# A fused attention and gated feed-forward kernel: first tile's first layer by halves of the contraction, tiny matmuls on zeros, four transpositions moved

## The chip, the core and the metric

The kernel runs on one core of a Trainium2 chip. The metric is the device time of one execution in microseconds (us). A core has TensorE (PE in the profile; PEld is its loading of weights), VectorE (DVE), ScalarE (ACT), GpSimd (POOL) and SyncE (SP), each with a queue of its own that it works through in order; they wait for one another by semaphores. Transfers are issued by GpSimd and SyncE here.

## What is computed

```python
scores = scale * np.matmul(q, k.transpose(0, 1, 3, 2))      # 8 batches, 8 heads, 576 rows, 64 columns
mask = (rel >= 0) & (rel < 64)                               # a causal window of 64
attn = softmax of scores under the mask
x = np.matmul(attn, v), heads side by side: 4608 x 512
gate = np.maximum(x @ w_gate, 0.0)                           # 512 x 1536
val = x @ w_val
return (gate * val @ w_out).astype(np.float32)               # 1536 x 512
```

## The kernel before, in words

The attention works on units of 192 rows; two units make a tile of the feed-forward part (384 rows for tiles 0 to 3, 512 for later ones). For a unit, TensorE makes scores in banks of PSUM (`u_st`, L265), ScalarE their exponentials (`u_exp`, L299), VectorE multiplies them by the mask (`u_mask`, L306; units 0 and 1 have a bias in the bank instead, `bias_mm`, L232), TensorE multiplies by v (`u_pv`, L336), VectorE divides (`u_recip`, L350, `u_norm`, L357) and transposes into the tile `xt` (`u_turn`, L379). In unit 1 ScalarE divides the second half of the heads (L369). `xt` has four slices of 128 along the contraction; heads 0 to 3 give slices 0 and 1, heads 4 to 7 slices 2 and 3.

The first layer of tiles 0 and 1 is `hidden` (L557). It goes over the 12 blocks of 128 columns of the two weights `wg` and `wv`: four matmuls (one for each slice, L589) fill a block's columns of a bank. ScalarE makes the relu of a `wg` bank (L572) and VectorE multiplies it by the `wv` bank (`gate`, L575). The banks of `hidden` are numbers 0 to 3 in turn (`one_bank`), and a bank is written again only when its relu or gate has read it. Tile 0 runs blocks 0 to 3 for its two units apart (192 columns, two blocks to a bank), then blocks 4 to 11 for both (384 columns, one block to a bank). Later tiles use another scheme (`fast_hidden`, L634), which multiplies fewer matrices.

Weights come in three parts of four blocks, each as two transfers issued by GpSimd (`w_load`, L159): slices 0 and 1, then slices 2 and 3. Ahead of some of them in GpSimd's queue stand copies that spread v over partitions (`v_spread`, L215).

The order of issue is written out by hand. `Weaver` holds a heap of actions with due times and a clock; each block of matmuls adds its estimated time (4 x (columns + 7) / 2400 us), and `W.advance` issues what has become due. `w_done` says when a part of the weights is taken to have landed: 15.2, 17.7, 20.3, 22.8, 27.0 and 29.6. The scores of unit 2 are due at 23.2, its exponentials at 24.0 and 0.4 apart, its masks at 24.45 and 0.4 apart, its values at 27.4; a relu or gate falls due when its bank's last matmul has been issued. The second batch's k and q are transposed by four instructions of VectorE (`qk_trans`, L199), due at 31.6 and 1.4 apart. The clock only fixes the order in each queue; when an instruction runs, semaphores and landings decide.

Before the first layer TensorE has matmuls on zeros (`keep_hot`, L229, and `heat`, L226): they add nothing to a result. The zeros are made by VectorE (L1088).

Of the kernel before, what the change touches and what calls it, by code (L numbers as in the profile page):

```python
# [47 lines left out]
def kernel(  # L48
# [10 lines left out]
    nc = tc.nc  # L59
# [4 lines left out]
    U = 192  # L64
    UB = S // U
    NU = B * UB
    NC = DM // 128
    NF = DF // 128
    G = 4
    scale = 1.0 / float(D) ** 0.5  # L70
    TT = 2 * U
# [55 lines left out]
    def band_bias():  # L127

        nc.vector.tensor_scalar(bias, mask, 30000.0, -30000.0, MUL, mybir.AluOpType.add)
        return 0.0  # L130
# [10 lines left out]
    W = Weaver()  # L141
    units = {}
# [3 lines left out]
    def xt_tile(t):  # L146
        if t not in xts:
            xts[t] = x_sb.tile([128, NC, WT], FP16, name="xt")
        return xts[t]


    w_done = {}

    def w_load(wt, src, f0, f1, landed):

        if wt is not wo:
            ns = slice(128 * f0, 128 * f1)
            for a in range(2):
                nc.gpsimd.dma_start(wt[:, 2 * a:2 * a + 2, ns], src.rearrange("(a p e) n -> a p e n", a=2, e=2)[a, :, :, ns])  # L159
        if wt is wo:  # L160
            nc.gpsimd.dma_start(wo[:, f0:f1], src.rearrange("(c p) n -> p c n", p=128)[:, f0:f1])
        w_done.update(((wt.name, f), landed) for f in range(f0, f1))

    def w_need(wt, f):
        while (wt.name, f) not in w_done:
            W.pop()
        W.advance(w_done[wt.name, f])

# [17 lines left out]
    def first_round(name, copies):  # L188
        n = S // 32 * D // len(copies)
        to = nat[0, name, 0] = nats[:, 2 * "kq".index(name)]  # L190
        for i, copy in enumerate(copies):
            copy(to[:, n * i:n * i + n], nat["32", name][:, n * i:n * i + n])

    def qk_trans(b, name, hh, j0=0, j1=S // 32):

        src = nat[b, name, hh].bitcast(FP32).rearrange("p (j e) -> p j e", e=32)
        dst = qTs[b % 2][:, hh] if name == "q" else kTs[b % 2][:, hh, 64:64 + S]
        dst = dst.bitcast(FP32).rearrange("p c o -> p (c o)")
        nc.vector.transpose(dst.rearrange("p (i j) -> p j i", i=32)[:, j0:j1], src[:, j0:j1])  # L199
# [23 lines left out]
    def heat(n, to, start=True):  # L223

        for _ in range(n):
            nc.tensor.matmul(to, zero[:, 0:128], zero[:, 0:to.shape[1]], start=start, stop=start, skip_group_check=not start)  # L226

    def keep_hot(to):
        nc.tensor.matmul(to, zero32[:, 0:128], zero32[:, 0:to.shape[1]], start=False, stop=False, skip_group_check=True)  # L229
# [6 lines left out]
    def one_bank():  # L236
        taken["one"] += 1
        to = singles[(taken["one"] - 1) % 4]
        while id(to) in unread:
            W.pop()  # L240
        return to
# [34 lines left out]
    def u_bias(u):  # L276

        st_tiles(u)
        for c in range(G):
            bias_mm(units[u]["st"][c])  # L280
        units[u]["biased"] = True
# [125 lines left out]
    def part_written(banks):  # L407
        written.update((id(to), 0) for to in banks)
# [145 lines left out]
        while normed[0] < n:  # L554
            W.pop()

    def hidden(t, spans, f0=0, f1=NF, each=1):  # L557

        if t not in gs:
            gs[t] = g_sb_p.tile([128, NF, WT], FP16, name="g_sb"), {}  # L560
        g_sb, done = gs[t]
        xt = xt_tile(t)
        n = spans[0][1] - spans[0][0]

        w = 512 // n
        each = max(each, w)

        def part(tile):
            return tile[:, 0:w * n].rearrange("p (w n) -> p w n", w=w)

        def relu(r_sb, h1):
            nc.scalar.activation(part(r_sb), part(h1), ACT.Relu)  # L572

        def gate(f, c0, r_sb, h2):
            nc.vector.tensor_tensor(g_sb[:, f:f + w, c0:c0 + n], part(r_sb), part(h2), MUL)  # L575
            done.update(dict.fromkeys(range(f, f + w), c0 + n))

        for fb in range(f0, f1, each):
            r2s = [f_sb.tile([128, 2, WT], FP32, name="pr", bufs=4) for _ in range(2)]
            r_sbs = {}  # L580
            for i, wt in enumerate((wg, wv)):
                for c0, f in ((c0, f) for c0, _ in spans for f in range(fb, fb + each, w)):
                    h = one_bank()
                    part_written([h])
                    for b in range(w):
                        W.advance(W.clock)
                        w_need(wt, f + b)
                        for c in range(NC):
                            nc.tensor.matmul(h[:, b * n:b * n + n], wt[:, c, (f + b) * 128:(f + b) * 128 + 128],  # L589
                                             xt[:, c, c0:c0 + n], start=(c == 0), stop=(c == NC - 1))  # L590
                        W.clock += 4 * (n + 7) / 2400.0
                    if i == 0:
                        r_sb = r_sbs[c0, f] = r2s[len(r_sbs) // 2][:, len(r_sbs) % 2]
                        W.at(W.clock, lambda r_sb=r_sb, h=h: relu(r_sb, h))
                    else:
                        W.at(W.clock, lambda f=f, c0=c0, r_sb=r_sbs[c0, f], h=h: gate(f, c0, r_sb, h))

    def fast_hidden(t, seven=None):

# [418 lines left out]
    def out_mm(t, op, sub, f):  # L1018
        g_sb, done = gs[t]
        while done.get(f, 0) < sub * 128 + 128:  # L1020
            W.pop()
        w_need(wo, f)
        nc.tensor.matmul(op, g_sb[:, f, bass.ds(sub * 128, 128)], wo[:, f],  # L1023
                         start=(f == 0), stop=(f == NF - 1))
        W.clock += 519 / 2400.0
# [48 lines left out]
    with tc.manual_schedule():  # L1074
# [14 lines left out]
        zero = zero32.bitcast(FP16)  # L1089
        st_tiles(0)  # L1090
        bands()
        v_load(0, ((1, 0, 128), (3, 0, 64)))
        v_load(1, ((3, 64, 128), (5, 0, 128)))
        w_load(*G3[0], 15.2)
        w_load(*V3[0], 17.7)
        k_zeros()
        band_bias()

        first_round("k", (dve, act))
        u_bias(0)  # L1100
        u_bias(1)
# [22 lines left out]
        for hh in range(2):  # L1124
            u_pv(1, (hh,), True)
        heat(1, units[1]["st"][3])
        for hh in range(2):
            u_recip(1, (hh,))
        u_norm_act(1, 1)
        u_norm(1, 0)  # L1130
        for hh in range(2):
            u_turn(1, (hh,))
        w_load(*G3[1], 20.3)
        w_load(*V3[1], 22.8)
        v_load(2)
# [13 lines left out]
        for u in (4, 5):  # L1149
            v_load(u)  # L1150
        for i, (name, hh) in enumerate((n, hh) for n in "kq" for hh in range(2)):
            W.at(31.6 + 1.4 * i, lambda name=name, hh=hh: qk_trans(1, name, hh))
        for hh, T in enumerate((36.6, 38.8)):
            W.at(T, lambda hh=hh: u_st(3, (hh,)))
            for i in range(G):
# [93 lines left out]
                pass  # L1249

        W.advance(15.3)
        hidden(0, ((0, U), (U, TT)), 0, 4, 4)
        hidden(0, ((0, TT),), 4, NF, 4)
        hidden(1, ((0, U),), each=4)
        output(0, (0, 1), (0, 8, NF))
        ready(1)
# [78 lines left out]
```

## Time and profile before

| | us |
|---|---|
| median of 3 runs | 302.06 (301.67 to 302.10) |
| the profiled execution | 302.04 |
| its span, first to last instruction | 300.3 |
| TensorE busy | 289.6 (96%) |
| VectorE busy | 251.7 (84%) |
| ScalarE busy | 196.0 (65%) |
| GpSimd busy | 201.7 (67%) |

A line of the timeline has the start and the length in us, the engine, the line of the kernel, the operation, what it writes and reads, the shape and the count of instructions merged; a bracket holds the engine's idle time before it and what ended that. The granted clock of TensorE is 1.0 throughout. In the window from 32 to 42 us TensorE is busy without a gap, and VectorE for 1.97 to 2.00 of every 2 us.

### The profile page before, as it was taken

To read this page: it belongs to the slowest core of one execution; us is meant where nothing else is said; L and a number is where in the kernel's file an instruction comes from. 1 tells how busy PE (TensorE), PEld (TensorE's weight loads), DVE (VectorE), ACT (ScalarE), POOL (GpSimd) and SP (SyncE) were. 2 spreads that over 40 slices of the span, in tenths; PEclk is the share of its full clock that TensorE was granted. 3 is DMA by queue.
4 is the path that set the end of the run, shared out by engine and by line. 5 is a ranking of instruction groups with operands and counts; after the bars stand their busy time and mean duration, and the time that the engine had idled before them with its cause. 6 is when DMAs were issued, how large, how long until landed. Compare 5 with 4: busy or idle time off the path is not lost.

```text
span 300.3 us, 11073 instructions
## 1 busy us (share of the span) xinstructions
PE 289.6 (96%) x4643; PEld 239.4 (80%) x4643; DVE 251.7 (84%) x517; ACT 196.0 (65%) x408; POOL 201.7 (67%) x241
## 2 busy tenths in 40 slices
PE   4899999999999999999999999999999999999994
PEld 2475877748957975888888888888888888888894
DVE  5947895997995999789999899989858985896584
ACT  3545336258848848885798579857985698538850
POOL 8767689868957893985957595759375617441750
PEclk9999999999999999999999999999999999999999
DMA  7999999979919636911399239922911210031013
GB/s 216 183 196 194 194 197 179 160 131 241 80 40 181 164 70 149 146 42 38 61 219 120 60 53 219 126 57 53 173 37 35 74 41 0 3 103 41 0 38 105
DMA packets 59506, 33.20 MB, mean 111 GB/s; under 512 B 39552, under 2 KB 53824, under 8 KB 59456
## 3 DMA queue, kind: packets, MB, share of 16 engines
q0 software_dynamic: 46688, 18.29, 52.3%
q1 hardware_dynamic: 12192, 13.75, 15.1%
q8 instruction: 36, 0.59, 0.8%
q10 hardware_dynamic: 576, 0.46, 0.5%
q14 instruction: 14, 0.11, 0.1%
HBM read 37.75 MB, written 9.44 MB: 157 GB/s over the span
## 4 chain that ended last, share of the span: by engine, by line
PE 87%; DMA 5%; POOL 4%; DVE 2%; issue 1%; DVEq 0%; POOLq 0%
PE bank L634 46%; PE bank L847 17%; PE bank L589 7%; PE bank L767 5%; PE bank L1023 5%; PE bank L265 3%; DMA wg<-in_moe_w_gate_dram 3%; PE bank L465 2%; DMA v<-in_v_dram 2%; POOL v L205 1%; PE bank L336 1%; POOL wg L159 1%; DVE g_sb L659 1%; DVE g_sb L797 0%; POOL wv L159 0%
## 5 line engine op out<-in xcount | busy, mean ns | idle before, releaser
L659 POOL TENSOR_TENSOR g_sb<-pr 128x512 f16<-128x512 f32 (+1 forms) x36 | 42.7, 1193 | 43.6 <-ACT pr L676 43.6
L670 DVE TENSOR_TENSOR pr<-bank,pr 128x512 f32<-128x512 f32 (+1 forms) x96 | 58.5, 649 | 3.6 <-PE bank L634 1.9
L653 ACT COPY pr<-bank 128x512 f32<-128x512 f32 (+1 forms) x96 | 49.1, 566 | 13.7 <-PE bank L634 13.5
L659 DVE TENSOR_TENSOR g_sb<-r,bank 128x512 f16<-128x512 f32 (+1 forms) x48 | 31.3, 652 | 23.8 <-ACT r L703 22.4
L847 PEld LDWEIGHTS <-g_sb 128*128 128x128 f16 x444 | 41.8, 98 | 5.2 <-issue 0.2
L634 PE MATMUL bank<-xc,vs 128*128 128x256 f16 (+1 forms) x288 | 41.3, 266 | 0.0
L634 PE MATMUL bank<-xc,us 128*128 128x256 f16 (+1 forms) x288 | 41.3, 266 | 0.0
L634 PEld LDWEIGHTS <-vs 128*128 128x128 f16 x384 | 36.5, 98 | 3.5
L634 PEld LDWEIGHTS <-us 128*128 128x128 f16 x384 | 36.5, 98 | 3.3
L205 POOL DMA_DIRECT2D v<-in_v_dram x41 | 34.7, 866 | 2.2 <-DMA nats<-in_q_dram 1.0
L676 ACT ACTIVATE pr<-pr 128x512 f32<-128x512 f32 (+1 forms) x48 | 29.3, 610 | 9.8 <-DVE pr L670 9.8
L703 ACT ACTIVATE r<-bank 128x512 f32<-128x512 f32 (+1 forms) x48 | 27.7, 577 | 4.8 <-PE bank L634 4.0
L634 PEld LDWEIGHTS <-wg 128*128 128x128 f16 x288 | 27.4, 98 | 3.2
L634 PEld LDWEIGHTS <-wv 128*128 128x128 f16 x288 | 27.4, 98 | 2.6
L634 PE MATMUL bank<-xt,wg 128*128 128x256 f16 (+1 forms) x192 | 27.5, 266 | 0.0
L634 PE MATMUL bank<-xt,wv 128*128 128x256 f16 (+1 forms) x192 | 27.5, 266 | 0.0
L797 POOL TENSOR_TENSOR g_sb<-g_sb,xus 128x512 f16<-128x512 f16 x24 | 27.1, 1148 | 0.0
L847 PE MATMUL bank<-wo,g_sb 128*128 128x256 f16 (+1 forms) x222 | 26.6, 270 | 0.0
L430 ACT ACTIVATE pw<-bank 128x512 f16<-128x512 f32 x48 | 25.3, 605 | 1.1 <-PE bank L265 0.7
L847 PE MATMUL bank<-wts,g_sb 128*128 128x256 f16 (+1 forms) x222 | 25.4, 270 | 0.2 <-DVE xw L484 0.2
L643 ACT COPY bank<-bank 128x512 f32<-128x512 f32 (+1 forms) x48 | 24.6, 553 | 0.0
L572 ACT ACTIVATE pr<-bank 128x384 f32<-128x384 f32 x24 | 11.9, 501 | 15.5 <-PE bank L589 12.5
(107 smaller groups left out, 559.8 us busy)
## 6 DMA issues: line engine op xcount, KB each, us to landing
out_dram<-o_sb SPq DMA_DIRECT2D x30, 256.0 KB, 3.1
nats<-in_k_dram POOLq DMA_DIRECT2D x15, 288.0 KB, 6.1
nats<-in_q_dram POOLq DMA_DIRECT2D x15, 288.0 KB, 8.0
v<-in_v_dram POOLq DMA_DIRECT2D x31, 128.0 KB, 8.2
v<-v SPq DMA_DIRECT2D x27, 66.0 KB, 2.7
v<-v SPq DMA_DIRECT2D x13, 132.0 KB, 2.5
wg<-in_moe_w_gate_dram POOLq DMA_DIRECT2D x6, 256.0 KB, 6.4
wv<-in_moe_w_val_dram POOLq DMA_DIRECT2D x6, 256.0 KB, 8.1
```

The source lines that it names most:

```text
L205: nc.gpsimd.dma_start(v16s[b % 2][lo:hi, g, :, 0:64], v[b, :, 64 * g - 64 + lo:64 * g - 64 + hi].rearrange("h p d -> p h d"))
L430: nc.scalar.activation(d["p"][g].rearrange("p n c -> p (n c)"), d["st"][g], ACT.Exp, scale=scale)
L589: nc.tensor.matmul(h[:, b * n:b * n + n], wt[:, c, (f + b) * 128:(f + b) * 128 + 128], xt[:, c, c0:c0 + n], start=(c == 0), stop=(c == NC ...
L634: nc.tensor.matmul(to[:, HT * m:HT * m + HT], w[:, k, 128 * m:128 * m + 128], x[:, k], start=(first and m == 0 and k == 0), stop=(k == 1), ...
L643: nc.scalar.copy(at[j, "B", i][:, 0:TW], at[j, "A", i][:, 0:TW])
L653: nc.scalar.copy(pr[:, i], at[j, "A", i][:, 0:TW])
L659: eng.tensor_tensor(gh[:, f:f + 2, h], pair(r), pair(v), MUL)
L670: nc.vector.tensor_tensor(pr[:, i], to[:, 0:TW], pr[:, i], ADD)
L676: nc.scalar.activation(pr[:, 0], pr[:, 0], ACT.Relu)
L703: nc.scalar.activation(r, to[:, 0:TW], ACT.Relu)
L797: eng.tensor_tensor(to, x, y, op)
L847: nc.tensor.matmul(at[key][:, QN * m * whole:QN * m * whole + n1 - n0], A[:, 128 * m:128 * m + 128], B[:, c, n0:n1], start=(first and m == ...
```

## The change

The first layer of tile 0 runs by halves of the contraction. A group takes its banks together, two for `wg` in blocks 0 to 3, four otherwise; first all its blocks get slices 0 and 1, then all get slices 2 and 3. Only the first matmul of a bank starts the accumulation for the whole bank. The halves have due times of their own in `w_done`, the first 1.3 before the second. Tile 1 runs as before.

Sixteen matmuls on zeros, with 4 columns of weights and 4 columns of data, go into the first bank of blocks 8 to 11 ahead of their first matmul. Another 112 of them stand ahead of the bias turns of unit 0. The four transpositions of k and q fall due at 31.9, 32.8, 34.4 and 35.8 instead of 31.6, 33.0, 34.4 and 35.8.

```diff
-        w_done.update(((wt.name, f), landed) for f in range(f0, f1))
+        w_done.update(((wt.name, f, a), landed - 1.3 * (1 - a)) for f in range(f0, f1) for a in range(2))
...
-            nc.tensor.matmul(to, zero[:, 0:128], zero[:, 0:to.shape[1]], start=start, stop=start, skip_group_check=not start)
+            nc.tensor.matmul(to, zero[:, 0:to.shape[0]], zero[:, 0:to.shape[1]], start=start, stop=start, skip_group_check=not start)
...
-    def hidden(t, spans, f0=0, f1=NF, each=1):
+    def hidden(t, spans, f0=0, f1=NF, each=1, halves=False):
...
+                items = [[(c0, f) for f in range(fb, fb + each, w)] for c0, _ in spans]
+                if halves and i == 1:
+                    items = [sum(items, [])]
+                for group in items if halves else [[item] for items_ in items for item in items_]:
+                    hs = [one_bank() for _ in group]
+                    part_written(hs)
+                    if (fb, i, n) == (8, 0, TT):
+                        heat(16, hs[0][0:4, 0:4])
+                    for cs in ((0, 1), (2, 3)) if halves else (range(NC),):
+                        for (c0, f), h in zip(group, hs):
+                            for b in range(w):
+                                W.advance(W.clock)
+                                w_need(wt, f + b, cs[-1] // 2)
+                                for c in cs:
+                                    nc.tensor.matmul(h[:, b * n:b * n + n], wt[:, c, (f + b) * 128:(f + b) * 128 + 128],
+                                                     xt[:, c, c0:c0 + n], start=(c == 0 and not (halves and b)), stop=(c == NC - 1),
+                                                     skip_group_check=halves)
+                                W.clock += len(cs) * (n + 7) / 2400.0
...
+        heat(112, units[0]["st"][0][0:4, 0:4])
         first_round("k", (dve, act))
...
-            W.at(31.6 + 1.4 * i, lambda name=name, hh=hh: qk_trans(1, name, hh))
+            W.at((31.9, 32.8, 34.4, 35.8)[i], lambda name=name, hh=hh: qk_trans(1, name, hh))
...
-        hidden(0, ((0, U), (U, TT)), 0, 4, 4)
-        hidden(0, ((0, TT),), 4, NF, 4)
+        hidden(0, ((0, U), (U, TT)), 0, 4, 4, True)
+        hidden(0, ((0, TT),), 4, NF, 4, True)
```

More of the change, by code (lines that the diff above doesn't have):

```diff
@@ L161, in w_load, with w_need @@
             nc.gpsimd.dma_start(wo[:, f0:f1], src.rearrange("(c p) n -> p c n", p=128)[:, f0:f1])
-        w_done.update(((wt.name, f), landed) for f in range(f0, f1))
-    def w_need(wt, f):
-        while (wt.name, f) not in w_done:
+        w_done.update(((wt.name, f, a), landed - 1.3 * (1 - a)) for f in range(f0, f1) for a in range(2))
+    def w_need(wt, f, a=1):
+        while (wt.name, f, a) not in w_done:
             W.pop()
-        W.advance(w_done[wt.name, f])
+        W.advance(w_done[wt.name, f, a])
     nat = {}
@@ L581, in hidden @@
             for i, wt in enumerate((wg, wv)):
[L582 to L596, printed above, removed]
+                items = [[(c0, f) for f in range(fb, fb + each, w)] for c0, _ in spans]
@@ new lines, in hidden @@
+                if halves and i == 1:
[15 more added lines that the diff above has]
+                                W.clock += len(cs) * (n + 7) / 2400.0
+                            if cs[-1] < NC - 1:
+                                continue
+                            if i == 0:
+                                r_sb = r_sbs[c0, f] = r2s[len(r_sbs) // 2][:, len(r_sbs) % 2]
+                                W.at(W.clock, lambda r_sb=r_sb, h=h: relu(r_sb, h))
+                            else:
+                                W.at(W.clock, lambda f=f, c0=c0, r_sb=r_sbs[c0, f], h=h: gate(f, c0, r_sb, h))
```

## The prediction

> **What bounds the kernel now.** The first slice of the page shows TensorE at 96% of the span, so a change at the start counts only through the idle time of TensorE that it takes away, or adds. The list of TensorE's waits gives nearly all of it:
>
> ```profile
> PE bank L232 <- DVE bias L129: 4.4, 1, 4.4
> PE bank L589 <- DMA wg<-in_moe_w_gate_dram: 0.7, 2, 0.4
> PE bank L589 <- DVE xt L379: 0.7, 1, 0.7
> ```
>
> The timeline of TensorE says where they lie (start, length, in brackets the idle time before):
>
> ```profile
> 13.84 0.33 PE L589 MATMUL bank<-xt,wg 128*128 128x192 f16 x2
> 14.51 1.33 PE L589 MATMUL bank<-xt,wg 128*128 128x192 f16 x14 [0.35 <-DMA wg<-in_moe_w_gate_dram]
> 16.50 1.48 PE L589 MATMUL bank<-xt,wg 128*128 128x192 f16 x16 [0.66 <-DVE xt L379]
> 20.45 2.76 PE L589 MATMUL bank<-xt,wg 128*128 128x384 f16 x16
> 26.24 0.49 PE L589 MATMUL bank<-xt,wg 128*128 128x384 f16 x2
> 27.09 0.50 PE L589 MATMUL bank<-xt,wg 128*128 128x384 f16 x2 [0.36 <-DMA wg<-in_moe_w_gate_dram]
> ```
>
> The first layer idles 0.35 + 0.66 + 0.36 = 1.37 us: the most that halves can save, since from 28 us on TensorE has no idle time worth naming. Starts in the timeline are one matmul's pitch apart: 0.083 us for 192 columns (16.50 to 17.82, 16 of them), 0.163 for 384 (20.45 to 23.07), 0.49 for a unit's scores or values. What evacuates the banks lies in the timeline of VectorE and of GpSimd:
>
> ```profile
> 24.56 0.56 DVE L575 TENSOR_TENSOR g_sb<-pr,bank 128x384 f16<-128x384 f32 x1 [3.28 <-PE bank L589]
> 25.03 0.98 DVE L306 TENSOR_TENSOR p<-p,mask 128x384 f16<-128x384 f16 x1
> 26.20 0.54 DVE L575 TENSOR_TENSOR g_sb<-pr,bank 128x384 f16<-128x384 f32 x1
> 26.67 0.35 DVE L306 TENSOR_TENSOR p<-p,mask 128x384 f16<-128x384 f16 x1
> 24.76 1.04 POOL L215 COPY v<-v 64x1024 f16<-64x1024 f16 x1
> ```
>
> A mask takes 0.35; the one issued at 25.03 took 0.98 and ended at 26.01, just behind GpSimd's copy (24.76 to 25.80). At 38.41 (0.79 for 0.25) and 40.55 (0.74) it is the same, each ending 0.11 to 0.12 behind a GpSimd operation. A gate, which reads a bank, isn't held (24.56 lies inside the copy from 24.10). Today the first gate of blocks 4 to 7 stands ahead of all masks, with the due times 24.445 and 24.45.
>
> **The halves, step by step.** Start 13.84: eight matmuls on the first half take 0.66, to 14.50; the second half landed at 14.47 (landings are an issue's start and its time to landing: 8.13 + 6.3 here, 17.31 + 8.5 and 18.00 + 9.0 for the last of wg, 19.07 + 9.3 and 20.34 + 9.3 for the last of wv), so the 0.35 goes and the group ends at 15.17. What is late next is unit 1's turn: its first half ends at 15.53, and 0.12 later (as 16.38 to 16.50 now) eight matmuls run to 16.31; the second half starts at 16.50 as before, but has 8 left, not 16: 17.16 against 17.82. The 32 of wv (2.66) end at 19.82, before 20.45: **-0.65**. Relus (0.38 apart) and landings (16.43, 17.51) are in time.
>
> Now four banks end together. Gates follow each other by 0.47 (27.20: two in 1.00); a gate starts 0.275 behind its bank's last matmul. They end at 19.64, 20.11, 20.58, 21.04, TensorE wants the banks at 19.82, 20.14 and 0.33 on: with 0.1 for the handover the fourth starts at 21.14, the second half ends 0.33 + 1.30 later, at 22.77, where now it is 23.15. Of the 0.65, **0.38** is left. Scores of unit 2 to 23.25, wv of blocks 4 to 7 (landed 22.34, 23.20) to 25.86.
>
> **Where it turns.** The clock that orders the issue is arithmetic: 15.3, plus 2 x 2.653 and 2.607, is 23.213; plus 0.58 for the scores, 23.793; the first halves of wv add 1.303. So the gates of blocks 4 to 7 fall due at 25.42, 25.75, 26.07, 26.40, and the masks, due 24.45, 24.85, 25.25, 25.65, come first: VectorE's queue becomes mask, mask, mask, gate, mask, gate, gate, gate. ScalarE makes the last relu at 23.13 and the exponentials end at 24.00, 24.37, 24.74, 25.11. Mask 0 runs at 24.05, ahead of the copy whose data land at 24.04; that copy then ends at 24.90, mask 1 at 25.19, the second copy at 26.1, mask 2 at 26.4, and the first gate only at **26.88**; mask 3 27.14, the other gates 27.61, 28.08, 28.55. TensorE waits 1.1 us for bank 0, not for the weights (landed 25.78). Blocks 8 to 11 then start at 27.38, 27.71, 28.18, 28.65 (16 tiny matmuls in front), unit 2's values end at 29.46, the second half at 30.76, wv (16 x 0.163) at 33.37. Now that point is 32.57: **+0.80**.
>
> Behind it VectorE is full until 45 us (2.00 of 2.00 in nearly every window of 2 us), and the four turns of k and q (1.24 each) stand between its gates. By the new times the first stands ahead of the gate of block 11 (clock 32.153: due 31.9 before 32.153). Gates end at 33.22, 33.68, 34.15, the turn at 35.31, that gate at 35.70; TensorE wants its bank at 35.36 and gets it at 35.80: **+0.43**. Today that gate ended at 34.33, 0.25 before the bank was wanted. The later masks and the last turn can add 0 to 0.5; I take 0, since the gate of tile 1's first block moves ahead of a turn in exchange. The turns issue nothing else; what waits for them is GpSimd's next load of k into the same tile (36.60, released by a turn), with the copies behind it. Its transfer lands at 48.8 and is wanted at the next turns, due 52.0, so a us of delay is hidden there.
>
> **The 16 tiny matmuls** stand between the gates of bank 0 (26.98) and bank 1 (27.71): 0.73 less the first block's 0.33 hides 0.40, or 25 ns each. Nearest rows: 7.5 ns (48 score matmuls in 0.36, four side by side) and 83 ns (192 columns), so 0 to 0.9 more on the path; I take 0.
>
> **The 112** wait for the zeros (VectorE to 2.43) and stand ahead of the bias turns, now at 4.41. Free are 1.9 us, 17 ns each. The same two rows bound them: 0.84 to 9.3 us. I take 20 ns, the row of small ones being nearer, so 0.3 late. The bias turns run at 0.320 each, twice 0.163, and end with the two on zeros at 8.34, while the scores wait for turned q until 8.33; nothing starts sooner for a faster clock, but eight turns at 0.163 would give back 1.26, so 33 ns each stay free if the clock comes up by then. Beyond that, the wait of 1.1 for bank 0 takes up as much again: 43 ns. Value: 0. The Trainium skill, "TensorE: Matmul & The Clock Gate", section "Wait — 56ns, not 53.3ns?", states a floor of about 25 ns from start to start however small a matmul is; by it, an estimate, the 112 take 2.8 us, within what is free only if the clock rises. No run here shows such matmuls yet.
>
> **The sum.** The profiled execution is 302.04 us with a span of 300.3; the median of the runs is 302.06. 302.04 + 0.80 + 0.43 = 303.27: **303.3**.
>
> **Rivals.**
> *The masks get by.* If VectorE keeps going past the waiting second copy, mask 2 ends at 25.45 and the first gate at 25.9, but mask 3 and the next gate still stand behind that copy (27.1): wv ends at 32.86, +0.29 + 0.43, **302.75**. If nothing holds the masks, wv ends at 32.20, -0.37 + 0.43: **302.1**. For the first: at 39.12 a mask followed a mask while a copy was due; against it, the three long masks above. The Trainium skill, "SBUF — State Buffer", section "SBUF: two separate sides", says that a VectorE operation with two SBUF inputs and a GpSimd operation that reads SBUF exclude each other, the one that starts first holding the port for its whole length. By that rule the second copy, due at 24.96, goes ahead of mask 2, due behind mask 1, and the 303.3 stands.
> *The waits go and nothing takes their place: faster.* Place: the queue of VectorE at 24 to 27 us. If the gates of blocks 4 to 7 end by 26.9 (all four ahead of the masks, as the first one is today), blocks 8 to 11 run from 25.9 to 27.2, the values to 27.7, second halves to 29.0 (landed 27.05), wv (28.33, 29.60) to 31.6: -0.97, **301.1**. For it: the landings allow it, and 1.37 is there to be had. Against it: the due times. It decides by the end of the fourth gate: 0.1 + 0.33 + 0.49 + 1.30 + 2.61 = 4.83 us are left behind it, so past 27.7 nothing is saved at 32.57.
> *The 112 are slow.* From 43 ns each they delay the first scores beyond what later waits absorb; at 60 ns, 17 x 0.112 = 1.9 on top: **305.1**. Against it: the row of small matmuls.
>
> **Chances.** Forecast 0.42; masks get by, 302.75, 0.12; unhindered, 302.1, 0.20; faster, 0.18; slow 112, 0.08. A measurement here tells 0.2% (0.6 us) from no change: slower 0.42 + 0.12 + 0.08 = 0.62, same 0.20, faster 0.18. The forecast's own range is 302.8 to 304.2 (0 to 0.9 for the tiny matmuls and the small waits). To leave out no more than 2 in 10 the range reaches to the faster case: 301.0 to 304.2; outside lie the slow 112 and the best of the faster case.
>
> **What would show it.** In the profile after: no wait on a wg landing in the first layer; wv of blocks 0 to 3 ending near 19.8; three masks ahead of the gate of block 4, one of them long and ending behind the second copy; TensorE's longest wait in the first layer near 25.9, released by that gate; a wait near 35.4 released by a gate behind a turn. The prediction is wrong if that gate ends before 25.9 (then 302 or less), or if the first scores start after 8.4 by more than 1 us.

## The result, and the profile after

The changed kernel takes **303.63 us** (median of six runs, 303.34 to 303.97) against 302.06 for the kernel before (301.64 to 302.16): a ratio of 1.0057, interval 1.0044 to 1.0070. The profiled execution has a span of 301.9 us, 1.6 more than before. TensorE's waits, the list that was read first for the kernel before (engine, line, releaser: total us, how often, the longest; L596 is the line that was L589):

```profile
PE bank L226 <- DVE wts L1098: 2.5, 1, 2.5
PE bank L265 <- DVE qT L199: 0.7, 1, 0.7
PE bank L596 <- DVE g_sb L575: 0.3, 1, 0.3
PE bank L596 <- DVE xt L379: 0.3, 1, 0.3
...
PE bank L226 <- DVE g_sb L575: 0.2, 1, 0.2
```

The waits for landings of `wg` are gone, and waits for gates (`g_sb`) have come. Yet the waits of the first layer add up to less than the 1.37 us of before, so this list alone can't explain a longer time. TensorE's timeline can:

```profile
2.48 2.94 PE L226 MATMUL bank<-wts 128*4 128x4 f16 x112 [2.48 <-DVE wts L1098]
5.36 2.74 PE L232 MATMUL bank<-bias,ident 128*128 128x384 f16 x8
9.28 0.55 PE L265 MATMUL bank<-qT,kT 32*128 32x64 f16 x48
14.97 1.48 PE L596 MATMUL bank<-xt,wg 128*128 128x192 f16 x16
16.72 1.67 PE L596 MATMUL bank<-xt,wg 128*128 128x192 f16 x16 [0.27 <-DVE xt L379]
18.23 2.80 PE L596 MATMUL bank<-xt,wv 128*128 128x192 f16 x32
20.87 3.07 PE L596 MATMUL bank<-xt,wg 128*128 128x384 f16 x16
24.35 2.77 PE L596 MATMUL bank<-xt,wv 128*128 128x384 f16 x16
27.29 0.54 PE L226 MATMUL bank<-wts 128*4 128x4 f16 x16 [0.17 <-DVE g_sb L575]
...
33.77 1.48 PE L596 MATMUL bank<-xt,wg 128*128 128x192 f16 x16
36.22 0.82 PE L596 MATMUL bank<-xt,wv 128*128 128x192 f16 x8 [0.30 <-DVE g_sb L575]
```

Read it as a balance against the kernel before:
- The first scores start at 9.28 (8.38 before), the first layer at 14.97 (13.84): **+1.13**, one execution of each.
- wv of blocks 0 to 3 starts at 18.23 (17.82): the two groups ahead of it now idle 0.27, not 1.01. **-0.72**, +0.41 in all.
- wg of blocks 4 to 7 takes from 20.87 to 23.87, 3.00 instead of 2.70 (20.45 to 23.15): **+0.30**, in small pieces that no list of waits names: the handover of four banks.
- wv of blocks 4 to 7 ends at 26.96, the next matmul starts at 27.29 and the weights' ones at 27.76. From 26.96 to the end of wv of blocks 8 to 11 at 33.77 are 6.81; before, 26.24 to 32.57 were 6.33, of which 0.36 a wait for `wg`. **+0.48**.
- That makes +1.20 at 33.77. The output layer starts at 43.39 for 41.77, +1.62, and this stays: the matmuls of tile 2 begin at 70.70 for 69.08.

The queue of VectorE shows the turn:

```profile
25.05 1.73 DVE L306 TENSOR_TENSOR p<-p,mask 128x384 f16<-128x384 f16 x3 [2.95 <-ACT p L299]
26.70 0.54 DVE L575 TENSOR_TENSOR g_sb<-pr,bank 128x384 f16<-128x384 f32 x1
27.16 0.35 DVE L306 TENSOR_TENSOR p<-p,mask 128x384 f16<-128x384 f16 x1
27.43 1.47 DVE L575 TENSOR_TENSOR g_sb<-pr,bank 128x384 f16<-128x384 f32 x3
...
34.53 1.25 DVE L199 STREAM_TRANSPOSE kT<-nats 128x576 f32<-128x576 f32 x1
35.62 0.54 DVE L575 TENSOR_TENSOR g_sb<-pr,bank 128x384 f16<-128x384 f32 x1
```

Three masks stand ahead of the gate of block 4, and take 1.73 in place of 0.35 + 2 x 0.27; of these the first alone takes 1.19 (25.05 to 26.24), beside two copies of GpSimd that fill 24.32 to 26.03:

```profile
24.32 1.71 POOL L215 COPY v<-v 64x512 f16<-64x512 f16 x2 [2.93 <-DMA v<-in_v_dram]
```

### The profile page after: what moved, and what is told of

Same layout as the page of the kernel before. It is cut to its first block, busy times and chain, and to the rows that moved or that the text cites. A ratio compares the mean times of both kernels' runs of the same rounds, so it can differ in the third digit from the quotient of the medians.

```text
span 301.9 us, 11330 instructions
## 1 busy us (share of the span) xinstructions
PE 293.5 (97%) x4771; PEld 242.4 (80%) x4771; DVE 251.7 (83%) x517; ACT 195.8 (65%) x408; POOL 201.1 (67%) x241
## 4 chain that ended last, share of the span: by engine, by line
PE 90%; DVE 4%; DMA 3%; issue 1%; ACT 1%; POOL 0%; DVEq 0%; ACTq 0%; POOLq 0%
PE bank L644 45%; PE bank L857 17%; PE bank L596 9%; PE bank L777 5%; PE bank L1033 5%; PE bank L265 3%; DMA nats<-in_q_dram 3%; PE bank L465 2%; PE bank L336 2%; DVE p L306 1%; DVE g_sb L669 1%; DVE g_sb L807 0%; DVE g_sb L575 0%; DVE qT L199 0%; ACT pr L572 0%
## 5 line engine op out<-in xcount | busy, mean ns | idle before, releaser
L205 POOL DMA_DIRECT2D v<-in_v_dram x41 | 34.6, 862 | 2.9 <-DMA nats<-in_k_dram 1.4
L713 ACT ACTIVATE r<-bank 128x512 f32<-128x512 f32 (+1 forms) x48 | 27.7, 578 | 4.8 <-PE bank L644 3.9
L807 POOL TENSOR_TENSOR g_sb<-g_sb,xus 128x512 f16<-128x512 f16 x24 | 27.1, 1148 | 0.0
L572 ACT ACTIVATE pr<-bank 128x384 f32<-128x384 f32 x24 | 11.0, 497 | 15.7 <-PE bank L596 12.8
```

Source lines behind the costliest of these rows:

```text
L205: nc.gpsimd.dma_start(v16s[b % 2][lo:hi, g, :, 0:64], v[b, :, 64 * g - 64 + lo:64 * g - 64 + hi].rearrange("h p d -> p h d"))
L713: nc.scalar.activation(r, to[:, 0:TW], ACT.Relu)
L807: eng.tensor_tensor(to, x, y, op)
```

## The experiments

Each kernel was timed beside the kernel before. "First scores", "first layer" and the like are starts in TensorE's timeline of the one profiled execution. Such an execution is one sample. The kernel before, e3, e1 and e5 do the same work ahead of the first layer and agree in the first scores (8.38, 8.33, 8.40, 8.35), and yet the first layer starts at 13.84, 14.37, 14.53 and 14.71; in the last three VectorE waits longer for v to land (0.46 to 0.60, 0.27 before). So the +1.13 above is measured against the earliest of four, and a difference under 0.9 us in that start proves nothing by itself.

### What the tiny matmuls cost: e1, e2, e7, e8

e1 is the changed kernel without the 112, e2 the kernel before with the 112 alone:

```diff
-        heat(112, units[0]["st"][0][0:4, 0:4])     # e1, from the changed kernel
+        heat(112, units[0]["st"][0][0:4, 0:4])     # e2, into the kernel before
```

> The changed kernel without the 112 tiny matmuls. Theory A (VectorE's queue at 24 to 29 us sets the end of the first layer): TensorE reaches blocks 8 to 11 about 1 us sooner and waits there for the first gate, which still stands behind three masks and the GpSimd copy; the wait of 0.17 us before it grows to about 1.1, and the time falls only by what that gate comes sooner, 0.1 to 0.5 us: about 303.3 us. Theory B (the 112 delay everything): the start moves back from 14.97 to 13.84 and all of it is kept: about 302.5 us.

> The kernel before with the 112 tiny matmuls alone. They end at about 5.4 us and the first scores start near 9.2 instead of 8.38. Theory A: the later start is partly taken up by the wait for the last part of wg at 27.09, where TensorE now stands idle from 26.57; it then comes at about 27.3 with all four matmuls of the block to do, not two: 0.4 to 0.7 us, about 302.6 us. Theory B: the whole delay of 0.9 to 1.1 us stays: about 303.1 us.

Both were missed, upward. e1: **304.51** (ratio 1.0087, 1.0071 to 1.0104), 0.9 slower than with the 112. e2: **306.57** (1.0153, 1.0123 to 1.0183), so the 112 alone cost 4.5 us, nearly three times what the whole change costs. In e2's list of waits stands a releaser that the kernel before hardly has:

```profile
PE bank L336 <- issue: 0.7, 1, 0.7
PE bank L847 <- issue: 0.6, 2, 0.5
```

"issue" is time in which TensorE waits for nothing that the profile shows. It lies far from the 112; the longest stands in front of the values of a later unit (0.46 more at 205 us):

```profile
57.02 0.43 PE L336 MATMUL bank<-v,p 128*32 128x65 f16 x32 [0.74 <-issue]
```

On the page of the changed kernel a DMA queue brings instructions (packets, MB, share of the engines):

```profile
q8 instruction: 37, 0.61, 0.8%
```

In the kernel before it has 36 packets and 0.59 MB, so a packet is 16 KB. A matmul counts as two instructions on TensorE, the load of its weights and itself (4643 + 4643 on the page of before). The changed kernel has 128 pairs more, 256 instructions, and one packet more: 64 bytes each. From this came a theory: TensorE's program arrives in blocks of 256 instructions; 112 + 16 = 128 pairs are one whole block, so everything behind them keeps its place in its block, while 112 alone move each later instruction by 224, and a block's end to where TensorE has no slack. e7 and e8 test it by numbers that are otherwise alike, ahead of the bias turns in the kernel before:

```diff
+        heat(128, units[0]["st"][0][0:4, 0:4])     # e7; 16 in e8
```

> The kernel before with 128 tiny matmuls at the front instead of 112. They take 16 x 25 ns = 0.4 us more than the 112. Theory F (instructions are fetched in blocks of 16384 bytes; 128 matmuls with their weight loads are 256 instructions, a whole block, while 112 are 224 and shift every later block boundary against the work): no wait of TensorE for its own instructions, and only the later start counts: 302.6 to 303.4 us. Rival (the time of the tiny matmuls itself makes the 306.6 of the 112 alone): 306.6 us or more.

> The kernel before with 16 tiny matmuls at the front. They end at 2.9 us, before the bias turns at 4.4, so that they delay nothing. Theory F (block boundaries): 32 more instructions move every later boundary by an eighth of a block; waits of TensorE for instructions may appear, anywhere from 0 to 2 us: 302.1 to 304 us. Rival (only time at the start counts): 302.0 us.

e7: **303.10** (1.0035, 1.0023 to 1.0047), as the theory says: 16 tiny matmuls more than in e2 make it 3.5 us faster, and the list of waits has no "issue". e8: **304.17** (1.0056, 1.0035 to 1.0076), but its nine runs fall into two groups, four at 302.81 to 303.13, as in e7, and five at 304.17 to 304.93. The profiled one is the slowest: its first load of q landed at 8.97, which made the first scores 11.00, and TensorE still ran at half pace at 15.50 (two matmuls on zeros in 1.50, which take 0.91 in the kernel before at 9.16). So e8 doesn't show that 16 cost more than 128. e1 (16 alone, 32 instructions) against e3 below (none), 304.51 to 303.35, and against the changed kernel (128), 303.63, goes with the theory; its profiled execution, the slowest of five, has a wait of 1.8 us at 59 us for copies of v that came late. So a whole block is far cheaper than a part of one in e7 against e2, and the other comparisons are weaker. The "issue" waits of e2 are 1.3 of the 3.1 us by which its profiled execution (305.14) is longer than that of before (302.04).

### What the masks and the halves cost: e3, e4, e5

e3 is the halves alone: neither group of tiny matmuls, and the four turns at their old due times.

> The halves alone, without tiny matmuls and with the old due times of the four turns. Theory A: the loss is that of the halves, with the gates behind the masks: about 303.2 us, between 302.7 and 303.7. Theory B: the halves gain what the waits for weights cost, 0.4 to 1.0 us: 301.1 to 301.7 us.

e3: **303.35** (1.0038, 1.0025 to 1.0052), as expected. The halves by themselves make the kernel slower, with waits for gates as forecast. But one thing stands out. The list puts a wait of 1.2 on the turn of `xt`, and the timelines of VectorE and of TensorE say that it was no such wait:

```profile
15.48 0.58 DVE L379 STREAM_TRANSPOSE xt<-xus 128x384 f16<-128x384 f16 x1
```

```profile
17.01 1.48 PE L594 MATMUL bank<-xt,wg 128*128 128x192 f16 x16 [1.16 <-DVE xt L379]
```

The half that these matmuls read was there at 16.06; they start 0.95 later. In e5 the same turn ends at 16.41 and they start at 16.77, with the second half done only at 17.26. In the changed kernel the turn ends at 16.67 and they start at 16.72. In e1, e3 and e5 one instruction packet starts at 14.5 to 14.6 us, 2.3 to 2.4 us ahead of that start; in the changed kernel the one near by starts at 15.7.

The kernel before has the same wait. The prediction read its 0.66 at 16.50 as the wait for the second half of unit 1's turn, but the first two of these matmuls read the first half, and that was there at 15.53:

```profile
14.95 0.58 DVE L379 STREAM_TRANSPOSE xt<-xus 128x384 f16<-128x384 f16 x1
```

In e2, with the same order of matmuls, two of the 16 start with the first half (they are counted in the 18) and only 14 wait for the second:

```profile
15.29 2.07 PE L589 MATMUL bank<-xt,wg 128*128 128x192 f16 x18
17.88 1.31 PE L589 MATMUL bank<-xt,wg 128*128 128x192 f16 x14 [0.52 <-DVE xt L379]
```

The count of instructions tells what it is. Ten starts of TensorE are late without data to explain it: the three "issue" waits of e2 (57.02, 173.65, 205.05), one of 0.26 in e12 below (17.07), the first matmul of the first layer in e8 (18.25), and the first one of unit 1 in the kernel before (16.50), e1 (17.03), e3 (17.01), e5 (16.77) and e7 (18.13). Twice the number of matmuls that the trace has ahead of each is 188 or 190 more than a multiple of 256, for all ten, and an instruction packet started 2.3 to 2.6 us earlier. So these are the ends of blocks, and TensorE had run out of instructions there, though the profile itself doesn't name it; at most other ends of blocks it goes on without a pause. A whole block (e7) leaves unit 1's wait where it was.

This bears on the halves. In the kernel before, wv of blocks 0 to 3 starts 3.98 behind the first layer (17.82 less 13.84); with the halves alone in e3 3.96 (3.37 in e5); with the 112 alone in e2 3.74; with both, in the changed kernel, 3.26. The 112 ahead move the block's end from unit 1's first matmul to the first of wv (18.23), and there the packet, started 2.6 us earlier at 15.67, comes in time. So the halves win at unit 1 what was expected of them only when the block's end lies elsewhere; each of these is one execution.

e4 is the changed kernel with the masks and values of unit 2 behind the gates of blocks 4 to 7:

```diff
-        plan_exps(23.2, 2)
-        plan_values(27.4, 2)
+        plan_exps(23.2, 2, False)
+        for i in range(G):
+            W.at(26.45 + 0.05 * i, lambda i=i: u_mask(2, i))
+        plan_values(28.9, 2)
```

e5 is e3 with the same edit, the new times of the turns, and the copies of v for units 4 and 5 due at 45.5 instead of 45.6.

> The changed kernel with unit 2's four masks due at 26.45 to 26.60 and its values at 28.9, so that the four gates of blocks 4 to 7 stand ahead of the masks and the values behind the four second halves. The computation is the same. Theory A: the first gate ends near 26.8 and the others 0.47 apart without a mask between them, TensorE goes through blocks 8 to 11 without the waits, and wv of these blocks ends about 0.5 to 0.7 us sooner than 33.77: about 303.0 us, since the 112 still set its arrival at 27.0. Theory B: the order of VectorE doesn't matter, the start does: 303.6 us.

> The halves without tiny matmuls, with unit 2's masks and values behind the gates (as in the kernel with the gates first), and the copies of v for units 4 and 5 due at 45.5 instead of 45.6, so that SyncE's queue has them ahead of the first output tile, as in the kernel before. The computation is the same. Theory A (the halves lose by what is late behind them, VectorE's order first): TensorE reaches blocks 8 to 11 near 26.5 and goes through them without a wait; wv of these blocks ends near 32.4 instead of 33.8; with the wait of 0.3 to 0.5 us for the gate behind the first turn: about 302.4 us. Rival (the order of VectorE costs nothing, something else in the halves does): 303.3 us as with the halves alone.

e4: **303.81** (1.0054, 1.0041 to 1.0067); e5: **303.28** (1.0037, 1.0024 to 1.0050). In both the wait at blocks 8 to 11 is gone, but e4 is 0.18 above the changed kernel and e5 0.07 below e3, both within the spread of their runs, so both came nearer to their rivals (303.6 and 303.3). From the start of wv of blocks 4 to 7 to the end of wv of blocks 8 to 11 e4 takes 9.12 (24.85 to 33.97) where the changed kernel takes 9.42; but q landed later in the profiled execution, and its first layer started at 15.47. e5's queue of VectorE first:

```profile
26.11 1.95 DVE L575 TENSOR_TENSOR g_sb<-pr,bank 128x384 f16<-128x384 f32 x4 [4.16 <-ACT p L299]
27.98 1.16 DVE L306 TENSOR_TENSOR p<-p,mask 128x384 f16<-128x384 f16 x4
```

Four masks in 1.16, so a mask that no copy accompanies isn't long. The other traces agree. In the five kernels whose masks start more than 0.2 us before GpSimd's second copy of v ends (before, changed, e1, e3, e6), the long mask ends 0.21 behind that copy in each; in the other nine every mask takes 0.34 to 0.36. e6 and e9 below have the changed kernel's order of masks and gates, but by chance the copies end later in e6, at 26.84, and in e9 the masks start only behind them (25.78). e6 first, then e9:

```profile
24.90 2.15 DVE L306 TENSOR_TENSOR p<-p,mask 128x384 f16<-128x384 f16 x3 [2.95 <-ACT p L299]
```

```profile
26.05 1.12 DVE L306 TENSOR_TENSOR p<-p,mask 128x384 f16<-128x384 f16 x3 [2.95 <-ACT p L299]
```

Counted from the start of wv of blocks 4 to 7, the first gate is done after 3.32 in e6, 2.89 in the changed kernel and 2.39 in e9, and TensorE waits for it 0.60, 0.17 and not at all. Then e5's TensorE:

```profile
18.08 2.80 PE L594 MATMUL bank<-xt,wv 128*128 128x192 f16 x32
20.72 3.07 PE L594 MATMUL bank<-xt,wg 128*128 128x384 f16 x16
...
24.20 2.77 PE L594 MATMUL bank<-xt,wv 128*128 128x384 f16 x16
26.82 3.08 PE L594 MATMUL bank<-xt,wg 128*128 128x384 f16 x16
...
33.07 1.48 PE L594 MATMUL bank<-xt,wg 128*128 128x192 f16 x16
```

No wait is named from 18.08 to 33.07, and yet that takes 14.99, where the kernel before takes 14.75 (17.82 to 32.57) with a wait of 0.36 in it. The two groups of `wg` take 3.00 and 3.01 (20.72 to 23.72, 26.82 to 29.83) for 16 matmuls that are 2.6 long without a pause. Each follows a group of `wv` whose four banks end together; gates free them 0.47 to 0.49 apart (four in 1.95), first halves of a bank ask for them 0.33 apart. So **the halves pay 0.4 twice**, for the wait of 0.36 that they take away. That is not all that e5 loses: its output layer starts at 42.98 for 41.77, 1.21 late, of which 0.26 stand at 18.08, 0.24 come from there to 33.07, and 0.71 behind it. Of these 0.71 the gate behind the first turn makes 0.34; the rest isn't explained.

### A copy of v issued late: e6

By the new clock the output's store was issued ahead of the copies of v for units 4 and 5, and the last of these landed at 56.70 (51.17 before), 0.14 ahead of the values that read it. In e1, where it landed at 59.19, TensorE waited 1.8 us. e6 is the changed kernel with those copies first:

```diff
-            W.at(45.6, lambda u=u: v_spread(u))
+            W.at(45.5, lambda u=u: v_spread(u))
```

> The changed kernel with the copies of v for units 4 and 5 due at 45.5 instead of 45.6, which puts them ahead of the first output tile in SyncE's queue. In the changed kernel the last of them lands at 56.70 and the values want it at 56.84; with the old order it should land near 52. Theory A (that queue order only takes the reserve): 303.3 to 303.6 us, no run with a wait at 57 to 59. Rival (the order in SyncE's queue is a main part of the loss): below 303.0 us.

e6: **303.90** (1.0057, 1.0044 to 1.0070). The late copies aren't what the change costs, and the rival falls. What the changed kernel has is little reserve: 0.14 us of slack.

### The start: e9, e10, e11, e12

The 112 outlast the release of the bias turns (4.36) by 1.0 us, and the first scores are 0.90 late. If the first makes the second, zeros written earlier mend both:

```diff
+        zero32 = wts.rearrange("p a f n -> p (a f n)").bitcast(FP32)[:, 0:384]
+        nc.vector.memset(zero32, 0.0)
         for i in range(2):
             v_fixed(i, nc.vector)
-        zero32 = wts.rearrange("p a f n -> p (a f n)").bitcast(FP32)[:, 0:384]
-        nc.vector.memset(zero32, 0.0)
```

e9 is the changed kernel with this; e10 has e4's edit and e6's as well; e11 is e10 with the turns due at 32.6, 33.4, 34.6 and 35.8; e12 is e7 with the zeros early.

> The changed kernel, with the zeros written by VectorE ahead of the constant columns of v, so that the 112 tiny matmuls can begin near 1.4 us instead of 2.48 and, at 25.4 ns each, be done at about 4.3, before the bias turns are released at 4.36. Theory S (what the 112 cost in the changed kernel is the 0.95 us by which they outlast the wait for the bias): bias turns start at 4.4, first scores near 8.4 instead of 9.28, first layer near 14.0; the masks then hold the gates of blocks 4 to 7 as before, so TensorE waits some 0.7 to 1.0 us at the first of blocks 8 to 11, and the total falls only by 0.2 to 0.6, to 303.0-303.4. Rival (the loss behind the start is not made by the 112 but by later landings of k, q and instructions): first scores stay at 9.1 or later and the total stays at 303.5 or above.

> The same, with the masks and values of unit 2 issued behind the gates of blocks 4 to 7 and the copies of v for units 4 and 5 due at 45.5, ahead of the output's store. If the three terms found so far (112 too late by 0.95, the gates behind the held masks, the boundary of the instruction blocks moved away) are the whole account, the start is as in the kernel before, the halves bring their gain, nothing waits at blocks 8 to 11, wv of blocks 8 to 11 ends near 32.0 (32.57 before), and with 0.3 left for the gate behind the turn the total is 301.6 to 302.0. Rival (the start stays late for another reason): wv ends at 33 or later, total 303 or above.

> The same as the one before, with the four turns of k and q due at 32.6, 33.4, 34.6 and 35.8, so that the first stands behind the gate of block 11. If the wait of 0.3 near 35 to 36 us is that turn ahead of that gate, it goes, and the time is 0.1 to 0.3 lower. Rival: both first turns now stand ahead of the first gates of tile 1, the wait moves there, and the time is the same.

> The kernel before, with 128 tiny matmuls ahead of the bias turns and the zeros written ahead of the constant columns of v. 128 at 25.4 ns from about 1.4 last to 4.65, 0.3 past the release of the bias turns. If all that the 128 cost at the front (303.10 for 302.09 with late zeros) is their length past that release, the time is 302.2 to 302.5 and the first layer starts near 14.1. Rival (the cost comes from instruction transfers beside the first loads): first layer at 14.8 or later and 302.8 or above.

e9: **303.47** (1.0062, 1.0039 to 1.0086); e10: **303.71** (1.0059, 1.0041 to 1.0078); e11: **303.61** (1.0055, 1.0035 to 1.0075); e12: **302.57** (1.0027, 1.0009 to 1.0045). The theory fell: in e9 the first scores come after 9.1, as its rival had it, and the total lies between the two. e9's TensorE:

```profile
1.43 2.94 PE L226 MATMUL bank<-wts 128*4 128x4 f16 x112 [1.43 <-DVE wts L1096]
4.40 2.72 PE L232 MATMUL bank<-bias,ident 128*128 128x384 f16 x8
...
9.14 0.55 PE L265 MATMUL bank<-qT,kT 32*128 32x64 f16 x48 [1.37 <-DVE qT L199]
```

The bias turns start at 4.40, as before; the scores still at 9.14, after 1.37 of waiting for turned q. What makes q late is in VectorE's timeline, here for the kernel before and then for e9:

```profile
4.71 0.55 DVE L192 CAST nats<-vs 128x576 f16<-128x576 f32 x1 [0.35 <-DMA vs<-in_k_dram]
```

```profile
5.48 0.50 DVE L192 CAST nats<-vs 128x576 f16<-128x576 f32 x1 [1.13 <-DMA vs<-in_k_dram]
```

The chain from there to the turn of q (7.07 before, 7.83 in e9) is the same and begins 0.77 later, with the landing of the first k. In the changed kernel it begins 0.35 later (cast at 5.06), waits 0.24 for ScalarE's half of the cast and has a second cast of 0.78 for 0.45: 0.90 together with the handovers. So with the 112 the scores are late, but not by the length of the 112. e12 gains 0.5 on e7, with first scores at 8.98 for 9.71 and the first layer at 15.03, as the rival had it; what is left to the kernel before is 0.56, where 0.1 to 0.4 was expected and 0.7 or more by the rival, so neither theory had it whole.

Two of these profiles need a reservation. In e9 and e10 the granted clock of TensorE fell to 0.5 for 3.4 us, from 13.83 and from 11.30, and in none of the other profiles did it fall there. So the first layer of e9, at 15.96, and of e10, at 15.50, are late by this too; e11, without it, starts at 15.03.

e10 and e11 have no wait for gates in blocks 8 to 11 and bias turns on time, and take what the changed kernel takes; in e10 wv of blocks 8 to 11 ends at 33.70, as its rival had it (33 or later). The 16 tiny matmuls, at 27.28, have no wait of TensorE to stand in there, but the handover of the banks behind them gets shorter: they and the 16 matmuls of `wg` take 3.18 together (27.28 to 30.46), where e5's `wg` alone takes 3.01. So they cost 0.17 of their 0.47. e11 shows its rival: the wait of 0.34 behind the first turn goes, and one of 0.33 for turned q comes at 38.70, where the scores of unit 3 stand. No version here beats the kernel before.

## Why the prediction was right, and where it was off

The time was forecast at 303.3 and is 303.63. VectorE's queue was as foretold, several sizes were off, and that the sum came so near is partly luck: two errors in front and behind cancel for the most part.

- **Signs.** Three of five showed: no wait for a landing of `wg`, the three masks, and the wait behind a turn. Two didn't: wv of blocks 0 to 3 was to end near 19.8 and ended at 20.87, and the longest wait of the first layer was to be that for the first gate, 1.1; it was 0.17, and one of 0.27 for the turn of `xt` was longer.
- **Right: the queue.** Three masks ahead of the gate of block 4, the first of them long and ending behind the second copy (26.24 behind 26.03; the prediction put the hold on the second and third), that gate ending at 27.24 (26.88 foretold); no wait for a landing of `wg`; a wait of 0.30 behind a turn (0.43). The rule that was cited from the Trainium skill ("SBUF — State Buffer", section "SBUF: two separate sides") agrees with the masks of 1.19 beside the copies and 0.29 behind them (four in 1.16, e5). The reverse shows too: in e1 and e6 a mask began just ahead of a copy, and that copy took 1.23 for 1.04 and 0.83 for 0.60. No edit moved the copies alone; that they hold the mask rests on the times of the 14 traces.
- **Right in size by luck: the gain of 0.65 at unit 1 and the first weights.** The changed kernel idles 0.72 less there. But the 0.66 at 16.50 was read as a wait for data, and it is the end of a block of instructions. With the halves alone it stayed (e3); it went in the changed kernel, where the 112 had moved the block's end away.
- **Right: the four banks.** From -0.65 to -0.38 was foretold for the handover in wg of blocks 4 to 7, 0.27; it took 0.30. **Missing:** the same handover in blocks 8 to 11, once no mask is in the way. The faster rival wanted the four gates done by 26.9. e5 has its queue, and there the fourth gate ends 3.86 behind the start of wv of blocks 4 to 7 (28.06 less 24.20): past the 27.7 from which nothing is saved, and from the rival's own start at 23.25 it would be 27.1. So 26.9 was out of reach, and the gain was at most 0.6 (27.7 less 27.1), for which no run had the start.
- **Mis-sized: the 112.** Step "Value: 0". They took 25 ns from start to start, 2.88 us to the start of the bias turns. The Trainium skill's "TensorE: Matmul & The Clock Gate", section "Wait — 56ns, not 53.3ns?", was right with its floor of 25, the 20 ns taken were not. But the step failed for another reason: it looked for the cost on TensorE alone, as time that the bias turns lose or win back. The bias turns run at 0.32 each whatever stands ahead of them (eight in 2.74, 2.72 before), so nothing was won back; and the scores hang on the first load of k, which the step never touched. Wv of blocks 0 to 3 started at 18.23, not at 17.17 (19.82 less 2.65): 1.06 of error. How much of it the 112 made is not shown: e1, without them, starts its first layer at 14.53 and wv of blocks 0 to 3 at 18.35. (The step's own sum has a slip: 1.9 and 1.26 us free are 28 ns for each of the 112, not 33; as nothing was won back, it changes nothing.)
- **Right in direction: what absorbs it.** A late start was to be taken up by the wait for bank 0, 1.1. Since gate 4 hangs on the copies and not on TensorE, it did take up most: from the start of wv of blocks 4 to 7 to that of blocks 8 to 11 are 6.82 (24.35 to 31.17), where 7.51 was written (23.25 to 30.76). Error of 1.06 in front, 0.03 at the four banks, 0.69 given back here: 1.20 where 0.80 was written.
- **Right: the 16 cost nothing**, as long as bank 1 is late anyway: its gate ends at 27.97, when the first half of block 8 would be waiting for it even without them. e10 shows the price without that cover, 0.17.
- **After 33.77**: 0.43 foretold, 0.42 measured (1.62 less 1.20), 0.30 of it the turn.
- **Not seen at all: the count of instructions.** 112 and 16 were weighed as two costs. They are one number, 128; the 112 without the 16 cost 4.5 us, the 16 without the 112 about 1.2 (e1 to e3, with late copies of v in e1's profile).

The rivals: "masks get by" falls (the gate stood behind them), "faster" by e5, and "slow 112" had the right place and the wrong reason, at 25 ns and not 43 or more. The condition "first scores after 8.4 by more than 1 us" was nearly met, at 0.9.

**Open**: why the first loads land later with the 112 running; what e2 loses beside its 1.3 us of "issue"; and why versions that take the single waits away (e4, e10, e11) are no faster than the changed kernel. The sum of the loss is read from timelines; no experiment wins it back piece by piece.

## What to carry to other kernels

Splitting a contraction so that work starts on half of its data makes several banks end together, and then the engine that empties them sets the pace: compare its time for one bank with TensorE's before counting the wait as saved. An instruction that computes nothing still has a place in the program: in a program that TensorE runs at 96%, count added pairs against the size of an instruction block, see where the ends of the blocks fall, and test an added group at several sizes before a time is put down to what it does. And when something is put into an idle stretch, follow the chain that ends the stretch, not the engine that idles. A wait that a list puts on some data is that only if the engine starts when the data is there: the 0.66 here ended 0.97 after the half that was needed.

## What the runs showed of the hardware

- A matmul with 4 columns of weights and 4 of data takes 25 ns from start to start with its load: the bias turns start at 5.76 behind 128 of them (e7) and at 5.36 behind 112.
- Tiny matmuls did not bring TensorE's pace up: with 2.9 us of them directly ahead, the eight bias turns took 2.74, and without 2.72, 0.32 each, half the pace of 0.163 that such matmuls have later. The granted clock, 1.0 "throughout" in the kernel before, is on record only from 8.14 us on.
- The granted clock can fall to 0.5 for 3.4 us in one execution and not in the next: it did in the profiled e9 and e10 and in no other of the 14 between its first record and 300 us.
- The first load of k (0.6 MB) took 3.8 to 3.9 us from issue to landing in the five kernels without a long run of tiny matmuls, and 4.1 to 4.6 in the nine with it. What the queues moved from 3 to 4 us doesn't part the two groups: 0.29 MB in e9, 0.33 in the kernel before, 0.34 in the changed one, with no packet of `q8` until 6 us. First scores: 8.33 to 8.40 (but for e8, whose load of q straggled) against 8.96 to 9.71. One profiled execution each; no cause is shown.
- VectorE's masks, which read two tiles of SBUF, are held by a GpSimd copy that is under way: the held one ended 0.21 behind the copy in all five kernels where they met.
- The instruction queue brings 16 KB at a time, 256 instructions by the count of pairs and packets. TensorE can stand still at the end of such a block, for up to 0.74 us in e2, at a place that the edit didn't touch; ten such stops lie 188 or 190 instructions past a multiple of 256.
